# Cosine attention with a highway layer: full-width q and k loads, heads paired across partition halves

## The chip, the cores and the metric

The kernel runs on one core of one Trainium2 chip. The metric is the device time of one execution in microseconds (us), lower is better. Times are medians over a few executions. An execution of a one-core program is called slow when it is over 1.5% above the fastest one of the same kernel in the same rounds; the comparisons use the others.

Names in the traces: PE is TensorE's matmul, PEld its weight load, DVE is VectorE, ACT is ScalarE, POOL is GpSimd, SP is SyncE, which issues most DMAs here.

## The reference, cut to what matters

```python
# q, k, v: (8 batches, 12 heads, 448 tokens, 64), float32
q_n = q / (norm(q) + 1e-6);  k_n = k / (norm(k) + 1e-6)
attn = softmax(q_n @ k_n.T / tau)              # per batch and head
x = (attn @ v).transpose(0, 2, 1, 3).reshape(3584, 768)
H = maximum(x @ w_h, 0)
T = sigmoid(x @ w_t + b_t)
return T * H + (1 - T) * x                      # the highway layer
```

## The kernel before

Four heads of a batch make a "quad", 24 quads in all. For each quad the kernel loads q and k, squares and sums them to get norms, scales them into fp16, turns them with TensorE (the first four quads) or with DMA transposes, multiplies QK on TensorE, takes exp on ScalarE, multiplies by v, and divides. As batches finish, the highway layer follows. A small scheduler in the kernel orders all instructions by estimated durations before they are emitted.

The parts that the change touches (cuts marked):

```python
# load_qk: four transfers a quad, each into 64 partitions (s = partition half)
for t in range(2):
    for s in range(2):
        half = st["raw", Q][64 * s : 64 * s + 64]
        if t == 0:      # q: two heads per half, 1792 B runs
            eng.dma_start(half[:, 0:NGQ]..., q[b, h0 : h0 + 2].rearrange("h (p c) d -> p h (c d)", c=C))
        else:           # k: four heads per half; 256 of 448 elements, so one token of seven is loaded twice
            eng.dma_start(half[:, NGQ:NG]...,
                k[b, 4 * qd : 4 * qd + 4].rearrange("a (p c) d -> p a (c d)", c=C)[:, :, 192 * s : 192 * s + 256])
...
# squares: q on ACT, k on POOL (on DVE for the first quad)
eng = "ACT" if t == 0 else ("DVE" if Q == 0 else "POOL")
...
# cast_v, once a quad: one cast over 128 partitions
nc.vector.tensor_copy(vm_b[Q % NV][:, :, 0:D]..., st["vr", b][:, 4 * qd : 4 * qd + 4, 0:192]...)
...
# QK: a pair of 64x128 matmuls per step (step 0, the first, in 64x64 quadrants)
for h in range(2):
    hp = slice(64 * h, 64 * h + 64)
    if ci == 0:
        for s in range(2):
            mm(hp, sp[64 * s : 64 * s + 64, h, 0:S], kT[hp, 4 * s + 3, 64:128], s)
    else:
        s, j = divmod(ci - 1, 3)
        mm(hp, sp[:, h, 0:S], kT[hp, 4 * s + j, :], s)
# exp: reads PSUM in order
nc.scalar.activation(e[...], st["sp", Q, ci][:, :, 0:S], AF.Exp, scale=inv_tau)
...
# store: two transfers of 64 partitions per output tile
for i in range(2):
    nc.sync.dma_start(rows, loc["o"][64 * i : 64 * i + 64, :])
```

Of the kernel before, what the change touches and what calls it, by code (L numbers as in the profile page):

```python
# [133 lines left out]
def kernel(  # L134
# [18 lines left out]
    C = 7  # L153
    NGQ, NGK = 2 * C, 16
    NG = NGQ + NGK
    GR = ((0, NGQ), (NGQ, NG))
# [34 lines left out]
    NV = 3  # L191
    vm_b = [const.tile([128, 12, 66], FP16, name=f"vm{i}") for i in range(NV)]
    vt_b = [const.tile([128, NQ, 2, 2, 66], FP16, name=f"vt{i}") for i in range(2)]
# [19 lines left out]
    def fill_v(i):  # L213
        def f():
            nc.vector.memset(vm_b[i][:, :, D : D + 1], 2.0)
            if i < 2:
                nc.vector.memset(vt_b[i][:, :, :, :, :], 0.0)
                for s in range(2):
                    nc.vector.memset(vt_b[i][64 * s : 64 * s + 64, :, s, :, D : D + 1], 2.0)
                nc.vector.memset(e_b[i][:, 14 * S : 14 * S + 64], 0.0)  # L220
        return f
# [13 lines left out]
    def load_qk(Q):  # L235
        b, qd = divmod(Q, NQ)
        ring, wait = P.buf("raw", N_RAW)
        pri = slot_t[Q] - 45
        st["ring_raw", Q] = ring
        got = []  # L240
        for t in range(2):
            for s in range(2):
                def f(t=t, s=s):
                    if t == 0 and s == 0:
                        st["raw", Q] = raw_p.tile([128, NG, D], FP32, name="raw")
                    half = st["raw", Q][64 * s : 64 * s + 64]
                    eng = nc.scalar if Q == 0 and t else nc.sync
                    if t == 0:
                        h0 = 4 * qd + 2 * s
                        eng.dma_start(  # L250
                            half[:, 0:NGQ].rearrange("p (h c) d -> p h (c d)", h=2),
                            q[b, h0 : h0 + 2].rearrange("h (p c) d -> p h (c d)", c=C),
                        )
                    else:
                        eng.dma_start(
                            half[:, NGQ:NG].rearrange("p (a c) d -> p a (c d)", a=4),
                            k[b, 4 * qd : 4 * qd + 4].rearrange("a (p c) d -> p a (c d)", c=C)[
                                :, :, 192 * s : 192 * s + 256
                            ],
                        )  # L260
                o = op("SP", 60 if Q == 0 and t else 480, pri + 0.01 * (2 * t + s), wait, f, size=720)
                wait = [o] if not got else wait
                got.append(o)
                ring.append(o)
        st["got", Q] = got

    def load_v(b):
        ring, wait = P.buf("vr", N_VR)
        st["ring_vr", b] = ring
        n = NQ if b == 0 else 1  # L270
        got = []
        for part in range(n):
            for par in range(2):
                def f(part=part, par=par):
                    if part == 0 and par == 0:
                        st["vr", b] = vraw_p.tile([128, NH, 256], FP32, name="vr")
                    hh = slice(part * NH // n, (part + 1) * NH // n)
                    nc.sync.dma_start(
                        st["vr", b][64 * par : 64 * par + 64, hh, :],
                        v[b, hh].rearrange("h (p c) d -> p h (c d)", c=C)[  # L280
                            :, :, 192 * par : 192 * par + 256
                        ],
                    )
                pri = slot_t[NQ * b + part] - (34 if b else 20) + 0.01 * par
                o = op("SP", 500, pri, wait, f, size=2000 // n)
                wait = [o] if not got else wait
                got.append(o)
                ring.append(o)
        st["gotv", b] = got
# [39 lines left out]
    def squares(Q):  # L329
# [6 lines left out]
        for t in range(2):  # L336
# [3 lines left out]
            def f(t=t, eng=eng):  # L340
                g0, g1 = GR[t]
                st["sq", Q, t] = sq_p.tile([128, g1 - g0, D], FP16, name=f"sq{t}")
                o, i = st["sq", Q, t][:, :, :], st["raw", Q][:, g0:g1, :]
                if eng == "ACT":
                    nc.scalar.activation(o, i, AF.Square)  # L345
                else:
                    (nc.vector if eng == "DVE" else nc.gpsimd).tensor_mul(o, i, i)  # L347

            a = op(eng, {"ACT": 750, "DVE": 1070, "POOL": 1900}[eng], due,
                   wait + st["got", Q][2 * t : 2 * t + 2], f, kind="lock" if eng == "DVE" else "")  # L350
            ring.append(a)
            st["ring_raw", Q].append(a)
            for part in range(2):
                def g(t=t, part=part):
                    n2 = nrm_tiles(b)[0]
                    g0, g1 = GR[t]
                    n = (g1 - g0) // 2
                    nc.vector.reduce_sum(  # L358
                        n2[:, qd, g0 + n * part : g0 + n * part + n],
                        st["sq", Q, t][:, n * part : n * part + n, :], axis=AX.X,  # L360
                    )
                r = op("DVE", 500 + 60 * t, due + 1, [a] + wait_n, g)
# [66 lines left out]
    def norms(Q, rs_op):  # L429
        b, qd = divmod(Q, NQ)  # L430
        due = slot_t[Q] - (16 if Q else 20)
        for t in range(2):
# [3 lines left out]
            def f(t=t, eng=eng):  # L436
                g0, g1 = GR[t]
                st["qn", Q, t] = qn_p.tile([128, 7 + t, 128], FP16, name=f"qn{t}")
                rs = nrm_tiles(b)[1]
                e = nc.vector if eng == "DVE" else nc.gpsimd  # L440
                n, m = ((1, C), (2, 4))[t]
                for a in range(n):
                    gg = slice(g0 + 2 * m * a, g0 + 2 * m * a + 2 * m)
                    e.tensor_mul(  # L444
                        st["qn", Q, t][:, m * a : m * a + m, :].rearrange("p c (h d) -> p h c d", h=2),
                        st["raw", Q][:, gg, :].rearrange("p (h c) d -> p h c d", h=2),
                        rs[:, qd, gg].rearrange("p (h c) -> p h c", h=2)
                        .unsqueeze(3).to_broadcast([128, 2, m, D]),
                    )

            a = op(eng, (1000 if eng == "DVE" else 1850) + 250 * t, due + t, wait + [rs_op] + st["got", Q], f,
# [6 lines left out]
            if by_pe(Q):  # L458
                ringp, waitp = P.buf("pt", 2)

                def g(t=t):
                    st["tp", Q, t] = p_ps.tile([128, C + t, 128], FP16, name="tp", tag="pt")
                    for c in range(C + t):
# [4 lines left out]
                def h(t=t):  # L468
                    st["qT", Q, t] = qt_p.tile([128, C + t, 128], FP16, name=f"qT{t}")
# [9 lines left out]
            else:  # L479
                def g(t=t):  # L480
                    st["qT", Q, t] = qt_p.tile([128, C + t, 128], FP16, name=f"qT{t}")
# [5 lines left out]
                z = op("SP", 1230, due + 2 + t, [a] + wait2, g, size=1400)  # L487
# [4 lines left out]
    def cast_v(Q):  # L492
        b, qd = divmod(Q, NQ)
        ring, wait = P.buf("vm", NV)

        def f():
            nc.vector.tensor_copy(
                vm_b[Q % NV][:, :, 0:D].rearrange("p (h j) d -> p h j d", j=3),
                st["vr", b][:, 4 * qd : 4 * qd + 4, 0:192].rearrange("p h (j d) -> p h j d", j=3),
            )  # L500
        got = st["gotv", b]
        o = op("DVE", 470, slot_t[Q] - 6, wait + [o_fv[Q % NV]] + (got[2 * qd : 2 * qd + 2] if b == 0 else got), f, kind="lock")
        ring.append(o)
        st["ring_vr", b].append(o)
        st["vm", Q] = (ring, o)

    def cast_vt(b):
        ring, wait = P.buf("vt", 2)
        outs = []
        for s in range(2):  # L510
            def f(s=s):
                nc.vector.tensor_copy(
                    vt_b[b % 2][64 * s : 64 * s + 64, :, s, :, 0:D],
                    st["vr", b][64:128, :, 192:256].rearrange("p (g s h) d -> p s g h d", s=2, h=2)[:, s],
                )
            o = op("DVE", 270, slot_t[NQ * b] - 6, wait + [o_fv[b % 2]] + st["gotv", b], f, kind="lock")
            ring.append(o)
            st["ring_vr", b].append(o)
            outs.append(o)
        st["vt", b] = (ring, outs)  # L520
# [5 lines left out]
    def quad(Q):  # L526
# [4 lines left out]
        ring_vm, o_vm = st["vm", Q]  # L531
        ring_vt, o_vt = st["vt", b]
        e = e_b[Q % 2]
        vm, vt = vm_b[Q % NV], vt_b[b % 2]
        exps = {}
        for ci in range(7):
            ring_s, wait_s = P.buf("sp", 2)

            def f(ci=ci):
# [4 lines left out]
                def mm(rows, o, lhsT, s):  # L544
                    nc.tensor.matmul(  # L545
                        o.rearrange("p (c x) -> p c x", c=C), lhsT=lhsT,
                        rhs=qT[rows, :, 64 * s : 64 * s + 64], start=True, stop=True,
                    )

                for h in range(2):  # L550
                    hp = slice(64 * h, 64 * h + 64)
                    if ci == 0:
                        for s in range(2):
                            mm(hp, sp[64 * s : 64 * s + 64, h, 0:S], kT[hp, 4 * s + 3, 64:128], s)
                    else:
                        s, j = divmod(ci - 1, 3)
# [299 lines left out]
```

## Time and profile before

| | before |
|---|---|
| time, median of 3 executions | 368.11 us (366.62 to 369.37) |
| span of the profiled execution (itself 358.55 us) | 356.8 us |
| busy: PE / DVE / ACT / POOL | 270.6 / 269.8 / 194.7 / 167.6 us |
| load queue, as a share of 16 DMA engines | 85.2% |
| read from HBM | 40.90 MB |

Two engines are busy for three quarters of the span and the DMA engines for 85%, so no single row names the limit. The stages do: the prediction shows the slices, the stretches, the waits and the chain.

### The profile page before, as it was taken

What the parts mean: (1) busy time and instruction counts of PE and PEld (TensorE: products, weight loads), DVE (VectorE), ACT (ScalarE), POOL (GpSimd) and SP (SyncE); (2) the same over time, 40 slices, a digit from 0 to 9 for tenths busy, and PEclk for the clock granted to TensorE, in tenths of its full rate; (3) what the DMA queues carried; (4) which work ended last, traced back from release to release, by engine and by line L of the source; (5) the groups of instructions that cost most, each with busy time, mean ns of one, the idle gap of its engine ahead of it and who ended that gap; (6) DMA issues with size and microseconds to landing.
All of it is one profiled execution on the core that took longest, in us unless ns stands there. A gap on an engine that the chain in (4) does not pass through costs nothing.

```text
span 356.8 us, 7367 instructions
## 1 busy us (share of the span) xinstructions
PE 270.6 (76%) x2876; PEld 154.4 (43%) x2876; DVE 269.8 (76%) x553; ACT 194.7 (55%) x253; POOL 167.6 (47%) x170
## 2 busy tenths in 40 slices
PE   0045546747788699899788998899389999997983
PEld 0023224533345155445345555455154564554551
DVE  2775558795777969899979998979956796666563
ACT  0243356856273488576667773686409757663110
POOL 0012538997239826963685269727930592000000
PEclk9999556875899799999999999999879999999999
DMA  7999999999997999999999999999764167112213
GB/s 185 211 235 217 224 228 238 242 203 233 213 223 130 208 199 229 179 226 203 243 211 199 212 240 174 233 240 230 105 101 101 47 126 127 48 46 58 76 45 88
DMA packets 78500, 62.21 MB, mean 174 GB/s; under 512 B 42625, under 2 KB 73345, under 8 KB 78466
## 3 DMA queue, kind: packets, MB, share of 16 engines
q1 hardware_dynamic: 77922, 61.23, 85.2%
q10 hardware_dynamic: 544, 0.52, 0.6%
q8 instruction: 22, 0.36, 0.4%
q14 instruction: 12, 0.10, 0.1%
HBM read 40.90 MB, written 11.01 MB: 145 GB/s over the span
## 4 chain that ended last, share of the span: by engine, by line
PE 33%; DMA 31%; DVE 19%; SPq 7%; POOL 5%; issue 2%; ACT 2%; POOLq 0%; ACTq 0%; DVEq 0%
PE pt L710 21%; DMA raw<-in_q_dram 15%; DMA raw<-in_k_dram 7%; PE u L583 6%; PE sp L545 5%; DVE th L751 5%; DMA vr<-in_v_dram 4%; DMA wst<-in_moe_w_t_dram 3%; DVE o L759 3%; DVE hm L735 3%; POOL sq L347 2%; SPq L250 2%; DMA out_dram<-o 2%; POOL qn L444 2%; SPq L482 2%
## 5 line engine op out<-in xcount | busy, mean ns | idle before, releaser
L561 ACT ACTIVATE e<-sp 128x896 f16<-128x896 f32 x168 | 147.5, 920 | 50.5 <-PE sp L545 49.1
L710 PE MATMUL pt<-w,xT 128*128 128x384 f16 x672 | 145.7, 335 | 19.4 <-DVE xT L690 8.0
L444 POOL TENSOR_TENSOR qn<-raw,rs 128x512 f16<-128x512 f32 (+1 forms) x69 | 94.7, 1405 | 9.9 <-DVE rs L409 6.8
L545 PE MATMUL sp<-qT,qT 64*128 64x448 f16 (+1 forms) x384 | 66.6, 395 | 29.4 <-ACT e L561 18.0
L710 PEld LDWEIGHTS <-xT 128*128 128x128 f16 x672 | 54.8, 99 | 62.0 <-issue 30.2
L347 POOL TENSOR_TENSOR sq<-raw 128x1024 f16<-128x1024 f32 x23 | 45.0, 1958 | 72.3 <-DMA raw<-in_k_dram 64.1
L583 PEld LDWEIGHTS <-e 128*128 128x128 f16 x1536 | 66.7, 103 | 25.7 <-issue 12.4
L583 PE MATMUL u<-vm,e 128*128 128x65 f16 x1152 | 71.6, 202 | 3.9 <-DVE x L644 3.9
L358 DVE TENSOR_REDUCE n<-sq 128x8 f32<-128x512 f16 (+1 forms) x96 | 58.5, 639 | 16.3 <-ACT sq L345 12.0
L583 PE MATMUL u<-vt,e 128*128 128x65 f16 x384 | 61.8, 200 | 0.0
L730 ACT ACTIVATE tt<-pt 128x384 f16<-128x384 f32 x56 | 27.4, 489 | 47.0 <-PE pt L710 46.9
L751 DVE SCALAR_TENSOR_TENSOR th<-tt,hm 128x384 f16<-128x384 f16 x56 | 47.3, 844 | 1.6
L545 PEld LDWEIGHTS <-qT 64*128 64x128 f16 (+1 forms) x384 | 17.4, 97 | 71.8 <-issue 56.1
L345 ACT ACTIVATE sq<-raw 128x896 f16<-128x896 f32 x24 | 22.8, 950 | 39.1 <-DMA raw<-in_q_dram 34.9
L735 DVE SCALAR_TENSOR_TENSOR hm<-pt,x 128x384 f16<-128x384 f32 x48 | 26.5, 552 | 16.4 <-PE pt L710 15.9
L759 DVE SCALAR_TENSOR_TENSOR o<-x,th 128x384 f32<-128x384 f16 x48 | 32.8, 683 | 0.5
L411 POOL TENSOR_TENSOR ta<-rs,n 128x90 f32<-128x90 f32 (+1 forms) x18 | 8.2, 456 | 42.2 <-DVE rs L385 41.8
L644 DVE SCALAR_TENSOR_TENSOR x<-u,rd 128x384 f16<-128x384 f32 x48 | 26.6, 554 | 1.0
L623 DVE RECIPROCAL rd<-u 128x6 f32<-128x6 f32 x48 | 9.1, 189 | 19.8 <-PE u L583 19.5
L464 PE MATMUL tp<-ident,qn 128*128 128x128 f16 x60 | 7.1, 287 | 20.5 <-DVE qn L444 19.5
L690 DVE COPY xT<-xp 128x768 f16<-128x768 f16 x28 | 15.4, 550 | 4.9 <-PE xp L686 4.7
L710 PE MATMUL pt<-bth,ones_row 128*128 128x384 f16 x56 | 18.9, 337 | 0.0
(40 smaller groups left out, 137.1 us busy)
## 6 DMA issues: line engine op xcount, KB each, us to landing
raw<-in_k_dram SPq DMA_DIRECT2D x46, 256.0 KB, 8.9
raw<-in_q_dram SPq DMA_DIRECT2D x48, 224.0 KB, 8.3
vr<-in_v_dram SPq DMA_DIRECT2D x14, 768.0 KB, 10.7
out_dram<-o SPq DMA_DIRECT2D x56, 192.0 KB, 3.0
wst<-in_moe_w_h_dram SPq DMA_DIRECT2D x6, 384.0 KB, 9.9
wst<-in_moe_w_t_dram SPq DMA_DIRECT2D x6, 384.0 KB, 10.8
vr<-in_v_dram SPq DMA_DIRECT2D x6, 256.0 KB, 7.5
qT<-qn SPq DMA_TRANSPOSE x40, 4.2
```

Of the source, the lines that this page charges most:

```text
L347: (nc.vector if eng == "DVE" else nc.gpsimd).tensor_mul(o, i, i)
L358: nc.vector.reduce_sum(n2[:, qd, g0 + n * part : g0 + n * part + n], st["sq", Q, t][:, n * part : n * part + n, :], axis=AX.X,)
L444: e.tensor_mul(st["qn", Q, t][:, m * a : m * a + m, :].rearrange("p c (h d) -> p h c d", h=2), st["raw", Q][:, gg, :].rearrange("p (h c) d ...
L545: nc.tensor.matmul(o.rearrange("p (c x) -> p c x", c=C), lhsT=lhsT, rhs=qT[rows, :, 64 * s : 64 * s + 64], start=True, stop=True,)
L561: nc.scalar.activation(e[:, o : o + 2 * S].rearrange("p (a n) -> p a n", a=2), st["sp", Q, ci][:, :, 0:S], AF.Exp, scale=inv_tau,)
L583: nc.tensor.matmul(u[:, slot, :], lhsT=e[:, o : o + 128], rhs=rhs, start=(kc == 0), stop=(kc == 3),)
L644: nc.vector.scalar_tensor_tensor(out=o, in0=i0, scalar=0.0, in1=i1, op0=ALU.bypass, op1=ALU.mult)
L710: nc.tensor.matmul(loc["pt", qi][:, :], lhsT=loc["xT"][:, cc, :] if cc < CC else ones_row[:, :], rhs=w_f[w_i][:, cc, ms] if cc < CC else b ...
L730: nc.scalar.activation(loc["tt"][:, ms], loc["pt", qi][:, :], AF.Tanh)
L735: nc.vector.scalar_tensor_tensor(out=loc["hm"][:, ms], in0=loc["pt", qi][:, :], scalar=0.0, in1=xf()[:, ms], op0=ALU.max, op1=ALU.subtract,)
L751: nc.vector.scalar_tensor_tensor(out=loc["th", mh][:, :], in0=loc["tt"][:, ms], scalar=1.0, in1=loc["hm"][:, ms], op0=ALU.add, op1=ALU.mult,)
L759: nc.vector.scalar_tensor_tensor(out=loc["o"][:, ms], in0=xf()[:, ms], scalar=2.0, in1=loc["th", mh][:, :], op0=ALU.mult, op1=ALU.add,)
```

## The change

The intent: in two short stretches of the trace before, which the prediction shows, loads into 64 partitions moved data at little over half the rate of a load into 128 (201 against 349 GB/s). So q and k of a quad each become one transfer over all partitions. The four heads are laid out as two "streams": partitions 0 to 63 hold the even heads, 64 to 127 the odd ones. k no longer loads a token twice. A head's tokens then sit in one half of the partitions, so QK is made in four 64x64 quadrants. v is loaded in two layouts, one shifted by half, in two large and two small transfers. The exp reads its PSUM tile with a stride, which puts the queries back in order and lets most stores be full-width. v is cast in six instructions per batch, four large and two small, all of them on 64 partitions.

The core of the diff:

```diff
-        for t in range(2):
-            for s in range(2):
-                ...four half-width transfers, see above...
+        for t in range(2):
+                eng.dma_start(
+                    st["raw", Q][:, NT * t : NT * t + NT].rearrange("x (h c) d -> x h (c d)", h=2),
+                    (q, k)[t][b, 4 * qd : 4 * qd + 4]
+                    .rearrange("n (p c) d -> (n p) (c d)", c=C)
+                    .rearrange("(h x) f -> x h f", x=128),
+                )
...
+        va_src = rows.rearrange("(i x) f -> x i f", x=128)[:, :, 192:448]
+        vb_src = rows[64 : 64 + 640].rearrange("(i x) f -> x i f", x=128)[:, :, 0:192]
...
+        for s in range(2):
+            for par in range(2):
+                    p = slice(64 * par, 64 * par + 64)
+                    src = st["va", b][p, :, 0:192] if par == s else st["vb", b][p, s : s + 6, :]   # (shortened)
+                    nc.vector.tensor_copy(vm[p, s, :, :, 0:D], src.rearrange("p i (j d) -> p i j d", j=3))
...
+                    for half in range(2):
+                        if ci == 0:
+                            s, c = half, 6
+                        else:
+                            s, j = divmod(ci - 1, 3)
+                            c = j + 3 * (half == s)
+                        nc.tensor.matmul(
+                            sp[64 * half : 64 * half + 64, h, 0:S].rearrange("x (c p) -> x c p", c=C),
+                            lhsT=kT[hp, c, 64 * s : 64 * s + 64],
+                            rhs=qT[hp, :, 64 * s : 64 * s + 64], start=True, stop=True,
+                        )
...
-                    st["sp", Q, ci][:, :, 0:S], AF.Exp, scale=inv_tau,
+                    st["sp", Q, ci][:, :, 0:S].rearrange("x a (c p) -> x a p c", c=C),
+                    AF.Exp, scale=inv_tau,
...
-                nc.vector.scalar_tensor_tensor(out=o, in0=i0, scalar=0.0, in1=i1, op0=ALU.bypass, op1=ALU.mult)
+                nc.vector.tensor_mul(o, i0, i1)
...
+                nc.sync.dma_start(out[r0 : r0 + 128, :], loc["o"][:, :])
```

## The prediction

> **What bounds the kernel now.** I began with the page's slices.
>
> ```profile
> PE   0045546747788699899788998899389999997983
> DVE  2775558795777969899979998979956796666563
> PEclk9999556875899799999999999999879999999999
> DMA  7999999999997999999999999999764167112213
> ```
>
> One slice is 8.9 us. The DMA engines are full from the second slice to the 28th (9 to 250 us). TensorE and VectorE are half empty for the first 100 us and about nine tenths busy after 150 us. The last quarter belongs to TensorE. The stretches put numbers on this (columns: stretch, its length, then busy us of PE, weight loads, DVE, ACT, POOL, then granted clock, DMA share, GB/s):
>
> ```profile
> 0.00:40.00 40.00, 11.43 (x110) 7.04 (x110) 21.93 (x63) 11.71 (x13) 6.29 (x11) 0.93 1.05 214
> 40.00:80.00 40.00, 22.80 (x276) 14.41 (x276) 30.11 (x67) 24.42 (x29) 29.27 (x38) 0.67 1.10 228
> 80.00:120.00 40.00, 28.71 (x262) 15.53 (x262) 29.52 (x53) 18.89 (x26) 25.40 (x25) 0.84 1.01 197
> 160.00:200.00 40.00, 35.03 (x409) 20.10 (x408) 35.96 (x70) 27.43 (x37) 22.02 (x21) 1.00 1.05 213
> ```
>
> PE idles 57 of the first 120 us and has a clock of 0.67 in 40 to 80. The DMA share stays above 1.0 at only 200 to 230 GB/s: the engines are occupied, not fast. Who waits for them is in the table of waits, and the chain that ended last agrees:
>
> ```profile
> POOL sq L347 <- DMA raw<-in_k_dram: 64.1, 12, 24.5
> ACT sq L345 <- DMA raw<-in_q_dram: 34.9, 11, 6.9
> ...
> PE 33%; DMA 31%; DVE 19%; SPq 7%; POOL 5%; issue 2%; ACT 2%; POOLq 0%; ACTq 0%; DVEq 0%
> ```
>
> In order of time that chain is almost pure DMA up to 71 us, DMA with POOL up to 181 us, then PE and DVE. The highway layer's first matmul starts at 89.8 us, since the last weight load is only issued at 81.4 us. So this is a load-bound first half feeding a compute-bound second half.
>
> I then took the packet records of the trace, by size. They are the DMA's cost table (sum = packets times mean, over 16 engines):
>
> ```
>  256 B (transposes)     38,400 packets, mean  29 ns, tenth percentile  18 ns: 70.5 us
> 1024 B (k and v)        24,576 packets, mean  84 ns, tenth percentile  46 ns: 128.6 us
> 1792 B (q)               6,144 packets, mean 122 ns, tenth percentile  74 ns: 46.9 us
> 3072 B (weights, out)    5,121 packets, mean 177 ns, tenth percentile 121 ns: 56.8 us
> ```
>
> The gap between mean and tenth percentile is the point. From 7.5 to 8.0 us a weight load over 128 partitions takes 133 ns per 3072 B packet at 349 GB/s. From 8.5 to 9.0 us q loads into 64 partitions take 159 ns per 1792 B at 201 GB/s. In the tail, where almost nothing else moves, the half-width stores still show a median near 210 ns against 121 at best.
>
> [...]two overlapping halves sometimes run fast (78 ns per q packet at 8.0 us, 350 GB/s), but over 20 to 240 us the rate stays near 220. [...]The trace has both forms of QK:
>
> ```profile
> L545 PE MATMUL sp<-qT,qT 64*128 64x448 f16 x288 | 57.0, 392 | 18.1 <-ACT e L561 18.0
> L545 PE MATMUL sp<-qT,qT 64*64 64x448 f16 x96 | 10.0, 407 | 11.3 <-DVE qT L473 6.0 <-DMA qT<-qn 5.3
> ```
>
> That is 57.0/144 = 0.396 us per pair and 10.0/24 = 0.417 us per four quadrants: four run together. [...]The new strided PSUM read is by ScalarE; no instruction in this trace reads PSUM with a large element step at any length, so it is untested.
>
> **The change part by part.**
>
> *Loads.* k loses the token loaded twice: 12,288 packets of 1024 B become 6,144 of 1792 B. v keeps 12,288 packets, half of them now 768 B. Together 25.17 MB become 22.0 MB. Nearly all are now full width, as are three quarters and more of the stores. Estimates from the trace's own best and mean values: q and k 12,288 x 90 ns / 16 = 69 us; v 6,144 x 55 and 6,144 x 45 = 38 us; weights and stores 5,120 x 140 = 45 us; transposes 35,840 (seven blocks for k, not eight) x 29 = 65 us. Sum 217 us against 303: 86 us less engine time. DMA stops being the bound.
>
> *SyncE queue.* q and k issues fall from 96 to 48, stores from 56 to 32, v rises from 20 to 32. At about 0.6 us each that is 36 us less queue time, some of it in front of loads.
>
> *POOL.* sq on 896 instead of 1024 elements: at 1.89 ns per element, 23 x 0.24 = 5.6 us less. The k scaling goes from 46 x 1.194 to 23 x 1.827 us: 12.9 us less. About 18 us less of 168.
>
> *VectorE.* v casts go from 24 x 724 ns plus 16 x 441 (24.5 us) to 32 casts of 64x1152 plus the same 16. The slope between 384 and 768 elements is small (420 to 550 ns minimum); I take 0.75 us clear and 0.95[...], so 37.5 us: 13 us more. k's reductions on 448 instead of 512 save 48 x 63 ns = 3 us. The scalar_tensor_tensor turned tensor_mul keeps its 554 ns[...]. Net 10 us more on an engine busy 270.
>
> *TensorE.* 144 pairs become fours: 144 x 0.02 = 3 us more. The four k transposes on PE drop a block each: nothing.
>
> *ScalarE.* exp reads with a step of 64 elements; if the read is free it stays at 920 ns x 168.
>
> *The sum.* In program order the highway layer starts after QK of five quads in both kernels. Before, that is 90 us. Loads at 320 to 340 instead of 220 GB/s would bring the same bytes in two thirds of the time; POOL needs some 5.3 us a quad and the weights sit behind raw buffers that POOL frees, so I put it at 65 us: 25 us gained. From 90 us on PE is busy 229 of 267 us (86%). With the remaining DMA waits gone, but VectorE longer, I expect 91%: 229/0.91 = 252 us, 15 us gained. The span becomes 65 + 252 = 317 us. Times are 368.1/356.8 = 1.032 of the profiled span: 327 us.
>
> **The rivals.**
>
> *ScalarE's strided read costs.* Were it half rate, exp would be about 1.67 us, 281 us in 168, and ScalarE with its 54 us of other work would be at 335: about 345 to 375 us in time. [...]One chance in eight.
>
> *VectorE takes over.* It is 90% busy in 160 to 200 already and gets 10 us more, with casts in blocks of six per batch that delay PSUM evacuation. 280 us at 90% plus some 15 us of start and tail is 326 us of span, 336 in time. For it: th averages 844 ns against 558 median[...]; a denser schedule meets POOL more often. Against: POOL has 18 us less.
>
> *The transfer was hidden anyway.* Bytes fall only 7%, and after 181 us the chain holds little DMA. If only the bytes counted, 7% of the DMA-bound 180 us is 13 us: 355 us. Against: the 201 against 349 GB/s above.
>
> *v comes later.* Its loads are now placed 14 instead of 34 us ahead of the batch, and all six casts wait for all four. If one is late, a batch stalls by some 5 us; eight such make 40. Against: v's landing took 7.5 to 10.7 us in a full queue.
>
> **Range and chances.** The middle of my mechanism and the VectorE rival is 327 to 336; the first pulls lower if the schedule tightens further (to 305), the strided read and late v pull up. I say 328, 306 to 352 for 8 in 10. Faster by over 2% (below 360.8) 0.90, within 2% 0.06, slower 0.04, the last two mostly the strided read.
>
> **What would show it.** 1792 B packets near 90 ns and over 300 GB/s while loads are outstanding, with DMA slices below 9 by 150 us; POOL's wait for k far under 64 us; the first highway matmul near 65 us; exp still at 920 ns; casts of 64x1152 near 0.75 to 0.95 us; QK fours at 0.42 us; the tail PE at 9 as before. The prediction is wrong if exp grows with its stride, if full-width packets stay above 120 ns, or if PE's idle time only moves from the first 100 us to waits on VectorE later.

The sum came to 65 + 252 = 317 us of span and 327 us of time. Two of its figures, and a chance beside them, are my estimates. The 0.95 us of a cast beside POOL is the one in the 37.5 us (32 x 0.95 + 16 x 0.441); the casts of 128x768 in the trace before took 724 ns in the mean, against 550 in the median. The 320 to 340 GB/s of the loads stand a little below the 349 and 350 of the short stretches. The one chance in eight for the strided read has nothing measured behind it; the 1.67 us there is 920 ns and once more 896 x 0.84 ns, where 0.84 ns an element is (920-489)/512, from ScalarE's activations of 896 and 384 elements in the trace before.

## More of the kernel before

The profiled execution is unusually quick. The time of an execution is its span plus 1.7 to 2.0 us in both kernels, so this trace is of a 358.55 us execution, while nearly all others of this kernel take 364 to 371. One later execution took 359.23. Why two of them were 8 us quicker is not known. Trace differences against this one understate what the change gains.

## The result, and the profile after

| | before | after |
|---|---|---|
| time, median of 4 executions | 367.37 us (366.27 to 369.37) | 349.64 us (349.07 to 351.53) |
| span of the profiled execution | 356.8 us | 347.9 us |
| busy: PE / DVE | 270.6 / 269.8 us | 269.2 / 288.8 us |
| busy: ACT / POOL | 194.7 / 167.6 us | 196.5 / 152.6 us |
| load queue's share of the DMA engines | 85.2% | 57.7% |
| read from HBM | 40.90 MB | 37.75 MB |

The ratio is 0.952, with a 95% interval of 0.946 to 0.958. Ratios here and below are made from the fast runs of both kernels in the same rounds, so they are not quite the ratio of the medians. The kernel gained 17.7 us, where I had forecast 40.

The slices of the kernel after, one digit per 8.7 us:

```profile
PE   0037387645988889988988869959997999997982
DVE  4799978996699999899899989988799766666663
PEclk9999588765899999998999989998999999999998
DMA  8979568729988165993885576735323441311112
```

The wall of nines in the DMA row is broken up: beyond the fourth slice single nines remain, in slices 10, 11, 17 and 18. The row of DVE is now mostly eights and nines from the third slice to the 31st. The stretches say it in numbers (stretch, its length, then busy us of PE, PEld, DVE, ACT, POOL, then granted clock, DMA share, GB/s):

```profile
0.00:40.00 40.00, 10.55 (x120) 6.43 (x120) 31.94 (x77) 13.41 (x15) 10.39 (x12) 0.94 0.92 312
40.00:80.00 40.00, 28.09 (x406) 17.59 (x407) 36.05 (x74) 29.23 (x35) 30.32 (x40) 0.76 0.60 192
80.00:120.00 40.00, 31.38 (x317) 17.18 (x315) 32.94 (x57) 22.52 (x30) 26.20 (x25) 0.88 0.82 221
160.00:200.00 40.00, 34.84 (x408) 19.40 (x405) 38.65 (x69) 27.98 (x37) 20.49 (x17) 0.96 0.68 184
```

In the first 40 us the loads run at 312 GB/s where they ran at 214. In 160 to 200 us DMA falls from a share of 1.05 to 0.68, but PE is no busier than before (34.84 against 35.03), and DVE is at 38.65 of 40. Over 40 to 240 us DVE's busy time is 181.8 of 200 us, against 166.1 before.

The table of waits and, below it, the chain that ended last by engine:

```profile
POOL sq L340 <- DVE n L350: 46.8, 6, 12.5
POOL sq L340 <- DMA raw<-in_k_dram: 30.2, 4, 15.4
ACT sq L338 <- DMA raw<-in_q_dram: 15.6, 3, 9.5
...
DVE 47%; PE 40%; DMA 5%; issue 4%; ACT 3%; SPq 0%; ACTq 0%; DVEq 0%
```

POOL's wait for k fell from 64.1 to 30.2 us, but in its place POOL now waits 46.8 us for the reductions on DVE (n, line 350) to free its buffer. DMA's part of the chain went from 31% to 5%, and DVE's from 19% to 47%. SyncE's queue shows the same: stores now wait 76.6 us for DVE's last instruction of a tile (63.3 the full-width ones, 13.3 the others), where they waited 45.2 us.

Why DVE has more to do is seen in its instructions. Here are the durations of some of them in the kernel after (minimum/median/maximum ns, then first and last start):

```profile
L742 DVE SCALAR_TENSOR_TENSOR th<-tt,hm x56: 518/558/2051, 88.4 to 342.2; 128x384 f16<-128x384 f16 x56
L726 DVE SCALAR_TENSOR_TENSOR hm<-pt,x x48: 537/558/560, 87.8 to 336.0; 128x384 f16<-128x384 f32 x48
L494 DVE CAST vm<-va x16: 741/757/2227, 14.7 to 260.3; 64x1152 f16<-64x1152 f32 x16
L350 DVE TENSOR_REDUCE n<-sq x96: 568/609/623, 5.1 to 252.2; 128x7 f32<-128x448 f16 x96
```

The medians are clear work. The maxima of th and of the cast are up to four times as long; those of hm and of the reduction are not. The timeline at one such place (start, duration, engine):

```profile
156.63 3.31 POOL L340 TENSOR_TENSOR sq<-raw 128x896 f16<-128x896 f32 x2
...
158.30 2.06 DVE L750 SCALAR_TENSOR_TENSOR o<-xtail,th 128x384 f32<-128x384 f16 x1
```

The 558 ns instruction o stands for 1.5 us and ends at 160.36, just after POOL's second multiplication ends at 159.94. I summed this over each trace: for every DVE instruction, its duration over the tenth percentile of the same line, tile and form, where that is over 100 ns. I call the sum "contact". In every trace all of it lies on instructions that overlap a POOL instruction.

| | DVE busy | sum of tenth percentiles | contact |
|---|---|---|---|
| before | 269.8 us | 258.2 us | 31.4 us |
| after | 288.8 us | 261.9 us | 46.4 us |

(The middle column adds durations of instructions that overlap a little: in the kernel after, 327 of 559 start before the one in front ends, 79 ns before in the mean. So the columns do not add up exactly.) DVE's own work grew by about 4 us and its contact by 15. These are 19 us together, which is the growth of its busy time.

The number of instructions that are held for over 100 ns did not rise: it is 46 before and 41 after. Each is held for longer, 0.68 us in the mean before and 1.13 after. The time in which both engines are busy at once is the same within a microsecond, 138.0 us before and 137.1 after. So VectorE was not held more often; each hold cost more. The change also makes POOL's scaling of k one instruction of 1.69 us (the median of that form), where it was two of 1.05. That may be a part of the reason; no run tests it.

The records of packets, as sums over 16 engines:

| packet | before | after |
|---|---|---|
| 256 B (transposes) | 29 ns, 70.5 us | 24 ns, 53.1 us |
| 768 B and 1024 B (v; before also k) | 84 ns, 128.6 us | 40 and 55 ns, 36.4 us |
| 1792 B (q; after also k) | 122 ns, 46.9 us | 86 ns, 66.4 us |
| 3072 B (weights, stores) | 177 ns, 56.8 us | 139 ns, 44.4 us |

The sums are 303 and 200 us. The DMA side of the change did what it was made for.

### The profile page after: what moved, and what is told of

Its sections match the earlier page's. It is cut to its first block, busy times and chain, and to the rows that moved or that the text cites. A ratio compares the mean times of both kernels' runs of the same rounds, so it can differ in the third digit from the quotient of the medians.

```text
span 347.9 us, 7848 instructions
## 1 busy us (share of the span) xinstructions
PE 269.2 (77%) x3160; PEld 156.0 (45%) x3160; DVE 288.8 (83%) x559; ACT 196.5 (56%) x253; POOL 152.6 (44%) x147
## 3 DMA queue, kind: packets, MB, share of 16 engines
q1 hardware_dynamic: 68530, 57.49, 57.7%
HBM read 37.75 MB, written 11.01 MB: 140 GB/s over the span
## 4 chain that ended last, share of the span: by engine, by line
DVE 47%; PE 40%; DMA 5%; issue 4%; ACT 3%; SPq 0%; ACTq 0%; DVEq 0%
PE pt L701 24%; DVE n L350 10%; PE sp L537 7%; DVE th L742 7%; DVE vm L494 6%; PE u L571 6%; DVE o L750 4%; DVE hm L726 4%; DVE x L637 3%; DMA raw<-in_q_dram 3%; DVE xT L681 2%; DMA raw<-in_k_dram 2%; DVE rs L371 2%; ACT e L548 2%; DVE w L296 2%
## 5 line engine op out<-in xcount | busy, mean ns | idle before, releaser
L432 POOL TENSOR_TENSOR qn<-raw,rs 128x896 f16<-128x896 f32 x46 | 82.9, 1830 | 7.1 <-DVE rd L608 3.0
L537 PE MATMUL sp<-qT,qT 64*64 64x448 f16 x672 | 68.3, 402 | 11.3 <-ACT e L548 5.6
L340 POOL TENSOR_TENSOR sq<-raw 128x896 f16<-128x896 f32 x23 | 41.6, 1813 | 77.2 <-DVE n L350 46.8
L350 DVE TENSOR_REDUCE n<-sq 128x7 f32<-128x448 f16 x96 | 56.0, 605 | 4.6 <-ACT sq L338 2.1
L742 DVE SCALAR_TENSOR_TENSOR th<-tt,hm 128x384 f16<-128x384 f16 x56 | 45.8, 817 | 2.0
L537 PEld LDWEIGHTS <-qT 64*64 64x64 f16 x672 | 20.2, 107 | 48.0 <-issue 37.6
L637 DVE TENSOR_TENSOR x<-u,rd 128x384 f16<-128x384 f32 x48 | 26.5, 553 | 0.8
L452 PE MATMUL tp<-ident,qn 128*128 128x128 f16 x56 | 6.0, 265 | 24.1 <-DVE qn L432 21.7
L681 DVE COPY xT<-xp 128x768 f16<-128x768 f16 x28 | 15.4, 550 | 7.1 <-PE xp L677 6.9
L403 POOL TENSOR_TENSOR ta<-rs,n 128x84 f32<-128x84 f32 (+1 forms) x18 | 7.5, 417 | 30.8 <-DVE rs L377 29.7
L494 DVE CAST vm<-vb 64x1152 f16<-64x1152 f32 x16 | 16.3, 1021 | 0.2
```

The costliest lines, as they stand in the source:

```text
L340: (nc.vector if eng == "DVE" else nc.gpsimd).tensor_mul(o, i, i)
L350: nc.vector.reduce_sum(n2[:, qd, g0 : g0 + C], st["sq", Q, t][:, C * part : C * part + C, :], axis=AX.X,)
L432: (nc.vector if eng == "DVE" else nc.gpsimd).tensor_mul(st["qn", Q, t][:, :, :].rearrange("p c (h d) -> p h c d", h=2), st["raw", Q][:, g, ...
L494: nc.vector.tensor_copy(vm[p, s, :, :, 0:D], src.rearrange("p i (j d) -> p i j d", j=3))
L537: nc.tensor.matmul(sp[64 * half : 64 * half + 64, h, 0:S].rearrange("x (c p) -> x c p", c=C), lhsT=kT[hp, c, 64 * s : 64 * s + 64], rhs=qT ...
L637: nc.vector.tensor_mul(o, i0, i1)
```

## The experiments

My theory after the result (theory A): loads are cured, and VectorE has become the limit, so that a microsecond of VectorE is a microsecond of time. VectorE is longer mainly because a denser schedule puts more of its instructions beside POOL's. (The count above already speaks against the word "more"; e1 bears on it too.) The rivals: the quadrants cost TensorE time; full width hardly matters and something else made the gain; the gain was lost in TensorE's start or in v's loads. All twelve runs were timed in three rounds beside the kernel before. Read from the traces, the order of instructions on every engine is that of the kernel after in e1, e2, e4, e7, e8 and e11, apart from the instructions that the edit adds or replaces. In e3, e5, e6, e9 and e14 the scheduler made a new order, and e15 has that of e3. What these runs show includes their new order. A few runs are left out of the ratios, though not of the medians and ranges. Except for two kernels, all results were correct.

### e1_half_qk: the kernel after, q and k in two half-width transfers each

```diff
-                eng.dma_start(dst, src)
+                for s in range(2):
+                    p = slice(64 * s, 64 * s + 64)
+                    eng.dma_start(dst[p], src[p])
```

> The changed kernel with each q and k load issued as two transfers of 64 partitions in place of one of 128; the same bytes, the same packets, the same order on every engine. Theory A (the full width is what freed the DMA, and VectorE is now the limit): 1792 B packets go from 86 back to about 125 ns, DMA time of these rises by some 30 us, the DMA is full again in the first 80 us, and the time rises, but by less than the 18 us that the whole change gave: 352 to 362 us. Rival B (the width does not matter, the fewer bytes gave the gain): packets stay near 86 ns, the time stays within 1% of 349.6 us.

Measured: 358.78 us (355.07 to 361.18), ratio 0.9726 (0.9653 to 0.9799). The bytes and the packet sizes are unchanged, but 1792 B packets take 122 ns instead of 86, the mean that they had before the change. POOL's wait for k goes back up to 43.8 us, and its wait for DVE falls:

```profile
POOL sq L343 <- DMA raw<-in_k_dram: 43.8, 7, 21.8
...
POOL sq L343 <- DVE n L353: 27.7, 4, 9.5
```

So full width of q and k is worth 9 of the 18 us here, with every engine's order unchanged. Half the gain is width; the rest may lie in fewer bytes, v, stores or the new order, which no run separates. The edit also adds 48 DMA issues, and their cost is within these 9 us.

VectorE's side is telling as well. DVE's busy time is 288.9 us and contact 46.9, against 288.8 and 46.4 in the kernel after. With the loads slowed about half of the way back, contact did not move towards the 31.4 us of before. So the rise in contact is not simply the result of freed loads. And 9 us came with no change of VectorE's busy time, so VectorE is not the only thing that moves the end.

### e2_cast_twice: each cast of v done twice

```diff
-                    nc.vector.tensor_copy(vm[p, s, :, :, 0:D], ...)
+                    for _ in range(2):
+                        nc.vector.tensor_copy(vm[p, s, :, :, 0:D], ...)
```

> The changed kernel with each of the 32 casts of 64x1152 issued twice, order unchanged: 32 x 0.76 to 0.97 us = 24 to 31 us more on VectorE, nothing more on any other engine. Theory A (VectorE is the limit from about 10 to 240 us): the time rises by 70% or more of that, to 367 to 381 us. Rival C (TensorE, or the order of waits, is the limit, with VectorE filling gaps): less than a third of it, under 360 us.

Measured: 382.75 us (380.36 to 385.14), ratio 1.0411 (1.0344 to 1.0479). DVE's busy time rose by 29.4 us (318.2 against 288.8), the span by 30.7 (378.6 against 347.9):

```profile
PE 278.2 (73%) x3160; PEld 160.4 (42%) x3160; DVE 318.2 (84%) x591; ACT 196.9 (52%) x253; POOL 158.1 (42%) x147
```

Of the 29.4 us, 6.2 are contact, and POOL's busy time rose by 5.5 us, though it got no more work. In this kernel a microsecond added to VectorE is about a microsecond of time. VectorE is the limit.

### e3_ksq_act: k's squares on ScalarE instead of POOL

```diff
-            eng = "ACT" if t == 0 else ("DVE" if Q == 0 else "POOL")
+            eng = "DVE" if t and Q == 0 else "ACT"
```

> The changed kernel with k's squares on ScalarE (23 x 0.95 = 22 us more there) in place of GpSimd (42 us less there); results the same; the order on the engines is planned anew. Theory A (46 us of VectorE's time in the changed kernel is its instructions standing still beside a GpSimd instruction, 15 us more than before, and VectorE is the limit): that excess falls by a quarter or more, to under 36 us, VectorE busy falls from 289 to about 277 us, the time falls by 6 to 14 us, to 336 to 344. Rival D (the excess is harmless waiting, or ScalarE's exps are pushed back by the squares): the time stays within 1% or rises to 350 to 358 us.

Measured: 331.63 us (331.42 to 335.05), ratio 0.9051 (0.8983 to 0.9119). This is the fastest kernel, 18 us faster than the changed one, and more than either theory gave it. POOL's busy time fell to 109.7 us, contact from 46.4 to 24.6, DVE's busy time from 288.8 to 267.9, the span by 18.4. The page's busy times, the chain and a late stretch:

```profile
PE 266.6 (81%) x3160; PEld 155.6 (47%) x3160; DVE 267.9 (81%) x559; ACT 215.0 (65%) x276; POOL 109.7 (33%) x124
...
PE 53%; DVE 30%; DMA 7%; issue 3%; ACT 3%; POOL 2%; SPq 1%; DVEq 0%; POOLq 0%; ACTq 0%
```

```profile
240.00:280.00 40.00, 40.00 (x503) 23.47 (x499) 27.72 (x61) 27.04 (x36) 3.67 (x2) 1.00 0.35 85
```

PE takes over the chain again and is busy for all of the 40 us from 240 on. VectorE's share of 40 to 240 us hardly changed (180.6 us busy, against 181.8): the same work was done earlier, and what was left for the time after 240 us fell from 75.1 to 56.7 us. A busy share alone would not have shown the difference. But the edit also changes the schedule: the scheduler reorders instructions, and k's reductions now wait for another engine. e11 deals with that.

### e4_pairs_wrong: QK in pairs again

```diff
+                    if ci:
+                        s, j = divmod(ci - 1, 3)
+                        nc.tensor.matmul(sp[:, h, 0:S]..., lhsT=kT[hp, j, :],
+                            rhs=qT[hp, :, 64 * s : 64 * s + 64], start=True, stop=True)
+                        continue
```

The pair reads keys of another head as well, so the result is wrong; the times of the instructions are those of pairs.

> Wrong on purpose: QK of steps 1 to 6 as pairs of 64x128 as in the kernel before (288 matmuls in place of 576), on the wrong keys; all else unchanged. Theory A (four quadrants run together and cost some 0.02 us more than a pair): TensorE busy falls by about 3 us and the time by 0 to 3 us, 346 to 350. Rival E (the quadrants' extra weight loads hold TensorE and are where the gain went): the time falls by 6 us or more, to under 344.

Measured: 348.95 us (346.75 to 352.48), ratio 0.9472 (0.941 to 0.9534); PE's busy time is 269.1 against 269.2, where I had expected 3 us less. The quadrants cost nothing that can be measured. This rival falls.

### e5_before_ksq: the same move of k's squares, in the kernel before

The edit is that of e3, made in the kernel before.

> The kernel before with the same move as in e3: k's squares on ScalarE in place of GpSimd. Theory A (the kernel before is held by its loads in the first half, so GpSimd's contact with VectorE matters only in the second): the gain is less than half of the 18 us that the move gave the changed kernel: 359 to 366 us against 368. Rival F (GpSimd beside VectorE costs both kernels alike, and has nothing to do with where the change's gain went): 346 to 354 us.

Measured: 367.05 us (366.41 to 368.34), ratio 1.0003 (0.9934 to 1.0072). Contact fell there too, from 31.4 to 20.3 us, and DVE's busy time by 8, yet the time did not move, where I had expected 2 to 9 us. The DMA share is still 1.04 to 1.13 up to 240 us. So while loads are the limit, freeing VectorE in this way was worth nothing. The new order is a rival that no run removes: the highway layer starts at 103.9 us here, against 89.8 in the trace of before, and may hide a part of a gain. With e3 this gives a table of two by two:

| medians, us | squares on POOL | squares on ScalarE |
|---|---|---|
| loads of before | 367.37 | 367.05 |
| loads of after | 349.64 | 331.63 |

The change is worth 18 us in the left column and 35 in the right one. The forecast of 40 us was nearly the right size for a kernel whose VectorE meets POOL less.

### e6_v_wide_cast: v in half-width transfers, two casts over 128 partitions

```diff
-   (va and vb: two full-width and two small transfers; four casts of 64x1152)
+   for s, par: nc.sync.dma_start(vr[64 * par : 64 * par + 64, s, :, 0:n], rows[s][:, :, lo : lo + n])
+   for s:      nc.vector.tensor_copy(vm[:, s, :, :, 0:D], vr[:, s, :, 0:192]...)   # 128x1152
```

> The changed kernel with v loaded in four transfers of 64 partitions straight into the half where it is needed, so that two casts of 128x1152 do what four casts of 64x1152 did: 31.1 us of cast becomes about 16 x 0.95 = 15 us, while v's packets slow to 60 to 85 ns from 40 and 55. Theory A (VectorE is the limit): VectorE busy falls by 14 to 18 us and the time by 10 to 20 us, to 330 to 340. Rival B2 (half-width loads undo it): the time stays within 1% of 349.6 or rises.

Measured: 344.69 us (340.92 to 350.3), ratio 0.9351 (0.922 to 0.9482). DVE's busy time fell by 19.1 us, as hoped, but the span by only 6.0, a miss. The casts and the wait that came back:

```profile
L480 DVE CAST vm<-vr x16: 742/748/2242, 19.0 to 254.3; 128x1152 f16<-128x1152 f32 x16
```

```profile
POOL sq L332 <- DMA raw<-in_k_dram: 55.4, 8, 18.8
```

A cast over 128 partitions has the same median as one over 64 (748 against 757 ns), so the changed kernel pays twice for v. But v's packets of 768 and 1024 B rose from 40 and 55 to 61 and 82 ns at half width, and POOL's wait for k from 30.2 to 55.4 us. The highway layer starts at 93.4 us, against 79.0 in the kernel after, and needs 248.6 us from there, against 268.9. So 20 us were gained once it ran, and 14 were lost before it. The slower loads are the likely cause of the loss; the new order may have a part in it.

### e7_sq_twice and e8_pool_memset: POOL made busier in two ways

```diff
 e7:                 e.tensor_mul(o, i, i)
+                    if eng == "POOL":
+                        e.tensor_mul(o, i, i)          # reads SBUF again
 e8:                 ....tensor_mul(o, i, i)
+                    if eng == "POOL":
+                        nc.gpsimd.memset(scratch[:, :], 0.0)   # only writes
```

> The changed kernel with each of GpSimd's 23 squares issued twice, order unchanged: 39 to 42 us more GpSimd work that reads and writes SBUF; GpSimd stays under 200 us busy. Theory A (contact with GpSimd holds VectorE): VectorE's excess rises from 46 to over 54 us, and the time by 8 to 20 us, to 358 to 370. Rival G (only the order of work on GpSimd counts, and its idle time swallows this): within 1%, under 353 us.

> The changed kernel with a fill of an unused tile on GpSimd after each of its 23 squares: GpSimd is held for a similar time (1 to 2 us each, to be read from the trace) but reads no SBUF. Theory A in its narrow form (VectorE stands still beside GpSimd instructions that read SBUF): VectorE's excess stays near 46 us for instructions with two SBUF inputs, and the time rises by less than half of what e7 shows. Rival H (any GpSimd work delays the scaled q and k, and that delay is the cost): the time rises as in e7, in proportion to the GpSimd time added.

Measured for e7: 376.36 us (373.83 to 379.7), ratio 1.0229 (1.0131 to 1.0327). POOL got 42.4 us of squares more; contact rose from 46.4 to 68.7 us, DVE's busy time by 21.7, and the span by 23.1. That is more than I expected.

Measured for e8: 365.72 us (364.81 to 367.8), ratio 0.997 (0.9896 to 1.0044). POOL got nearly the same time in fills:

```profile
L343 POOL MEMSET scratch<- 128x2048 f16 x23 | 42.7, 1855 | 0.0
```

Contact rose to 67.9 us, DVE's busy time by 13.9, the span by 15.8. A version of my theory in which only POOL's reads of SBUF count falls: the fill costs 16 us where the second multiplication costs 27. But which instructions were held beside a fill is telling. From the two traces (stretched by over 100 ns, of those that overlap POOL by over 60 ns; each counts under the kind of POOL instruction that it overlaps longest):

| VectorE instruction | beside POOL arithmetic (after) | beside a fill (e8) |
|---|---|---|
| two inputs in SBUF: th, o, ta | 23 of 37 | 0 of 8 |
| one SBUF input: casts of v and w, integer tensor_scalar | 18 of 32 | 15 of 16 |
| a PSUM input, or a reduction | 0 of 163 | 5 of 41 |

Beside a fill, casts and scalar operations were held nearly always (15 of 16) and an instruction with two SBUF inputs never, though only eight were beside one. (Six more, all held, overlapped a fill too, but arithmetic for longer.) The five exceptions in the last line are 4 us together. All five start behind a tensor_scalar that is itself held, and end with it, to within the trace's 10 ns. Three of them are at one place:

```profile
120.53 1.46 DVE L374 TENSOR_SCALAR rs<-n 128x84 int32<-128x84 int32 x1
120.64 1.35 DVE L353 TENSOR_REDUCE n<-sq 128x7 f32<-128x448 f16 x1
```

So I take them as queued, not held. Such overlapping waits are counted twice in e8's contact. Counted once, it is 62.1 us, 15.7 more than after, which is near DVE's 13.9; in e7 nothing changes. The rival in which any POOL time counts alike, as a delay of POOL's own work, falls in that strict form too: 42.7 us of fills cost 16 us, 42.4 us of multiplications 27.

### e9_ksq_v: e3 and e6 together

The edits are those of e3 and e6.

> e3 and e6 together: k's squares on ScalarE, and v in four half-width transfers with two casts of 128x1152. If VectorE were still the only limit, its busy time falls from 268 to about 250 us and the time from 331.6 to about 315. If TensorE (267 us busy, 100% in 240 to 280 us of e3) and the slower v loads take over, as e6's small gain suggests: 325 to 333 us.

Measured: 341.14 us (338.62 to 343.82), ratio 0.9307 (0.9198 to 0.9417): 9.5 us slower than e3, and both expectations missed. DVE has 253.4 us, 14.5 less than in e3, but:

```profile
PE 53%; DMA 20%; DVE 15%; ACT 6%; issue 2%; SPq 1%; ACTq 0%; DVEq 0%
```

```profile
80.00:120.00 40.00, 28.59 (x314) 15.92 (x309) 32.47 (x64) 27.36 (x36) 24.40 (x26) 0.91 1.09 254
```

DMA's part of the chain is 20%, against 7% in e3, and in 80 to 120 us its share is 1.09. The doubled casts of the change are the price of v's full width, and once VectorE is relieved that price seems worth paying; e3 and e9 differ in their order as well.

### e11_sq_short_wrong: POOL squares 128 elements of 896

```diff
-                    (...).tensor_mul(o, i, i)
+                    nc.gpsimd.tensor_mul(o[:, 0:2, :], i[:, 0:2, :], i[:, 0:2, :])
```

The reductions of k read the tile of q's squares, so that nothing unwritten is read; a third buffer of squares keeps that from deadlocking. The order of instructions on every engine is that of the kernel after.

> Wrong on purpose (k is scaled by q's norms): the changed kernel with every instruction in its old place and order on all five engines, but GpSimd squares 128 of the 896 elements, about 0.3 us in place of 1.8, and the reduction reads q's squares instead. ScalarE gets nothing more. Theory A (GpSimd's occupancy beside VectorE is the cost, and e3's new order and ScalarE's extra load had no part in its gain): VectorE's excess falls from 46 to under 34 us and the time by 12 to 22 us, to 328 to 338. Rival D (e3 gained by its new order): under 5 us, 345 to 351.

Measured: 332.69 us (330.03 to 333.42), ratio 0.904 (0.8955 to 0.9124). This is e3's time without e3's order and with ScalarE's load unchanged (196.2 us busy). POOL's busy time is 120.8 us, contact 26.5, DVE's busy time 268.9. So a new order is not needed for e3's gain. The edit shortens POOL's squares, and it also takes them out of k's way: the reductions of k no longer wait for POOL. Which of the two counts more, the shorter occupancy or the missing wait, this run does not separate.

```profile
L343 POOL TENSOR_TENSOR sq<-raw 128x128 f16<-128x128 f32 x23 | 11.3, 493 | 66.2 <-DMA raw<-in_k_dram 66.2
```

POOL's long wait for DVE is gone, and POOL waits for loads again, which is no loss: it is idle because it is ahead.

### e14_ksq_xt: e3, and ScalarE also takes the copies of xT

```diff
-            nc.vector.tensor_copy(loc["xT"][:, :, :], loc["xp"][:, :, :])
+            nc.scalar.copy(loc["xT"][:, :, :], loc["xp"][:, :, :])
```

> e3, and the copies of the transposed x (28 of 128x768, 15.4 us on VectorE) on ScalarE, at about 0.8 us each. If VectorE is still the limit of e3 in 80 to 240 us: 5 to 12 us less, 320 to 327 us. If ScalarE's exps get in the way of these copies, or TensorE is the limit: 329 to 340 us.

Measured: 333.7 us (332.21 to 337.69), ratio 0.9067 (0.8977 to 0.9157). DVE went from 267.9 to 254.6 us and the time did not fall. This fits e3's chain, in which PE has 53%: VectorE alone is no longer the limit. That the copies on ScalarE (232.2 us busy, against 215.0), or the new order, took back a gain is not excluded.

### e15_ksq_half_qk: e3 with q and k at half width

The edits are those of e1 and e3.

> e1 and e3 together: k's squares on ScalarE, and each q and k load split into two half-width transfers. In the changed kernel the split cost 9 us while VectorE was the limit. Theory A (VectorE beside GpSimd hid part of what the loads gave): with that limit lifted the split costs more, 15 to 28 us over e3's 331.6: 347 to 360 us. Rival I (the two effects are independent): it costs 9 us again, 338 to 343 us.

Measured: 347.02 us (344.05 to 348.49). There is no ratio: one run of the kernel before took 359.23 us in these rounds, so its other runs, at 365 to 367, were slow. Beside e3, from other rounds and another chip, it is 15.4 us slower, with the same order on every engine. So q's and k's width is worth about 15 us where VectorE is relieved, and 9 where it is not. The time lies at the lower edge of what theory A expected (347 to 360), but outside the 338 to 343 of two independent effects.

### The runs together

| kernel | time, us | span | DVE busy | contact | POOL busy |
|---|---|---|---|---|---|
| before | 367.37 | 356.8 | 269.8 | 31.4 | 167.6 |
| after | 349.64 | 347.9 | 288.8 | 46.4 | 152.6 |
| e2, casts twice | 382.75 | 378.6 | 318.2 | 52.6 | 158.1 |
| e7, squares twice | 376.36 | 371.0 | 310.5 | 68.7 | 195.4 |
| e8, fill | 365.72 | 363.7 | 302.7 | 67.9 | 196.3 |
| e6, wide casts | 344.69 | 341.9 | 269.7 | 40.0 | 152.1 |
| e3, squares on ScalarE | 331.63 | 329.5 | 267.9 | 24.6 | 109.7 |
| e11, short squares | 332.69 | 331.4 | 268.9 | 26.5 | 120.8 |

From after to e2, e7, e8, e3 and e11, DVE's busy time moves by +29.4, +21.7, +13.9, -20.9 and -19.9 us and the span by +30.7, +23.1, +15.8, -18.4 and -16.5. Two runs leave this line, and both narrow loads: e6 (-19.1 and -6.0) and e1 (+0.1 and +9.1).

## Why the prediction was right or wrong, point by point

**What bounds the kernel now** held. e5 supports it: in the kernel before, VectorE was relieved of 8 us and the time did not move, with the rival of its order that is named there.

**Loads** were right: 200 us of engine time against the 217 forecast, 1792 B packets at 86 ns against 90, and waits for k halved. The 201 against 349 GB/s were read from stretches of half a microsecond; from 7.0 to 7.5 us the same full-width weight load ran at 221 GB/s. e1, with 122 against 86 ns over all packets, is the firmer evidence. The tell-tale that I named, DMA slices under 9 by 150 us, is only partly there: the row still has nines at the 17th and 18th slice (139 to 157 us), with gaps before them.

**SyncE queue**: the issues fell as counted, but the queue now waits for VectorE. No run isolates what the saved issues are worth.

**POOL** got 15 us less, where I had said 18: the squares fell by 3.4 us (45.0 to 41.6) and the scaling by 11.8 (94.7 to 82.9).

**TensorE** was right: a four of quadrants takes 68.3/168 = 0.407 us against 0.396 for a pair and 0.417 for the fours before, and e4 shows no cost. **ScalarE** was right: exp kept its duration with the strided read (917 ns with a step of 64 elements, 917 in order), so that rival fell without an experiment:

```profile
L548 ACT ACTIVATE e<-sp x168: 909/917/977, 25.0 to 313.4; 128x896 f16<-128x896 f32 x168
```

```profile
L561 ACT ACTIVATE e<-sp x168: 899/917/962, 24.3 to 322.7; 128x896 f16<-128x896 f32 x168
```

The first line is of the kernel after, the second of before; the medians are the same.

**VectorE** was mis-sized. The step "Net 10 us more on an engine busy 270" measured 19. The casts are not at fault: 31.1 us for 32 and 7.0 for the 16 small ones, 38.1 against the 37.5 forecast. Own work grew by about 4 us, less than I said, but contact grew by 15, and I had put down none beyond the casts' own 0.2 us each. From before to after, contact rose on the small instructions of the reciprocal root (rs and ta, 3.8 to 10.5 us), the casts of v (4.3 to 8.6), o (6.4 to 9.9) and the casts of weights (0.5 to 2.7); on th it even fell (16.5 to 14.9). A third of the rise, 5.3 us, is in the first 40 us, where before there was none. I had argued that POOL's 18 us less would count against it. Neither POOL's busy time nor the number of meetings explains the rise: 41 instructions were held, against 46, but for 1.13 us each, against 0.68. Beside POOL's scaling the holds went from 31 (19.2 us) to 22 (27.8 us), beside its squares from 8 (10.9 us) to 15 (18.0 us). Freed loads are not the simple reason either, since contact stays at 46.9 in e1. POOL's longer scaling of k, and the new order, are left as candidates; the cause of the longer holds is open.

**The sum is the step that failed.** It said: "With the remaining DMA waits gone, but VectorE longer, I expect 91%", and put the highway's start at 65 us. In the trace its first matmuls come at 79 us, and it runs steadily from 85 us, when the last weight has been cast. From 85 us on PE is busy 229.8 of 263 us: 87%, hardly more than the 86% of before. In place of the DMA waits came waits on VectorE, which is busy for 91% of 40 to 240 us. The two parts of the sum shrank from 25 and 15 us to some 5 to 11 and 4. e3 shows that the second part was there to be had: it starts its highway layer no earlier (83.7 us), yet needs about 246 us from there, less than the 252 that I had forecast. The start at 65 us appeared in no run; the earliest is 74.2 us, in e11. What would bring it is open.

The factor of 1.032 from span to time was also wrong. It compared the span of a 358.55 us execution with the median of others. The true step is 1.7 us, so my own forecast of the span, 317 us, meant 319 us of time. So the miss is larger than the 22 us between 328 and 349.64: in span the forecast was 31 us low (317 against 347.9), and the range, centred 8 us too high for its own working, held the result only just.

**The rivals.** "VectorE takes over" is what happened, but not in the way that was written there, "a denser schedule meets POOL more often": VectorE was held less often, and for longer. I gave it 280 us of VectorE at 90% and 336 us of time. VectorE has 288.8 us, and the time was 349.64, since VectorE idles 41 us outside 40 to 240 us, where I had allowed some 15 us of start and tail. I then averaged this rival with my main case, where I should have followed it to its end: before, VectorE was at 90% in 160 to 200 us already, so removing DMA's limit there could give no more than a tenth.

"The transfer was hidden anyway" fell with e1: width alone is worth 9 us. "v comes later" rested on a misreading of the diff: the lead of 34 us stays for all batches but the first, whose lead goes from 20 to 14.

**Where the missing gain went**, then: it was not lost in the loads. Of the 35 us that the change is worth with k's squares on ScalarE, 18 are missing while POOL makes them (e3, e11). How POOL itself running late and VectorE's standing share those 18 us is not wholly separated, since e3 and e11 change both. e2, which gives POOL no more work, shows that VectorE's time moves the end about one for one. DVE's 20 us less in e3 and e11 would then be enough for all of the gain.

The account of the held instructions goes no further than their counts. A PSUM input or a reduction: 0 of 163 held beside POOL's arithmetic in the kernel after, and 5 of 41 beside a fill, all queued as above. Two SBUF inputs: 23 of 37 beside arithmetic, 0 of 8 beside a fill. Casts and integer tensor_scalars: 18 of 32 beside arithmetic, 15 of 16 beside a fill. The timeline above shows one whole instruction held, 2.06 us for 0.56. Why the kinds differ was not shown.

## What to carry to other kernels

Before removing one limit, look in each stage for the engine that is next to it: an engine at 90% under a limit of 100% leaves a tenth to be gained, and what runs beside it may take the rest (contact rose by 15 us here). Price that as contact, by summing durations over their undisturbed value, and look at the length of a hold and not only at the number of holds: here fewer holds cost 15 us more. When a change gives less than forecast, try to move the new disturber: here one line, which the change itself did not have, doubled the gain to 9.5% (e3), and the same line before the change gave nothing.
